# One half of a hand-ordered attention and gated-unit kernel in another order, its closing test cut in two

## The chip, the cores and the metric

The kernel runs on one core of a Trainium2 chip. Its engines work side by side, each through its own list of instructions, in order: PE (matrix products into PSUM, with PEld, its weight loads), DVE (the vector engine, VectorE), ACT (the scalar engine, ScalarE, with exponential, tanh and copies), POOL (GpSimd, elementwise work in SBUF) and SP, which here only issues transfers. PSUM has eight banks, numbered 0 to 7. The metric is the device time of the whole program in microseconds, lower being better, as the median of three runs.

## The reference

Eight batches of eight heads, 576 positions, head width 64. Attention is causal, and every head has a decay made of running sums of a gate `s`:

```python
scores = scale * np.matmul(q, k.transpose(0, 1, 3, 2))
cum = np.cumsum(np.maximum(s, 0.0), axis=-1)
bias = -(cum[:, :, :, None] - cum[:, :, None, :])
scores = np.where(causal, -1000000000.0, scores + np.minimum(bias, 0.0))
attn = softmax(scores)                      # over keys
x = (attn @ v)                              # (batch, 576, 512)
gate = sigmoid(causal convolution of x over positions, 5 taps per channel)
out = (gate * (x @ w_val)) @ w_out
```

## The kernel before

The work is cut into 32 blocks `n`, each one batch and one pair of heads (`n // 4` is the batch, `n % 4` the pair). The names of steps are those of the code; a number behind the dot is the block, or the batch and a part of it.

- `ld_q`, `ld_k`, `ld_v`, `ld_t` load on SP's queue (lines 435, 467, 471, 458); `c_q`, `c_k` cast queries and keys to bf16, `qt`/`qq` turn them over on PE and `qe` copies them out of PSUM (`tt`, `te` the same for the last 64 positions). `vp` (line 474, POOL) multiplies the values by the decay's factor.
- `s0`, `s1`, `s2` are the score products of a block in three portions (line 505), each on a pair of banks; `e0`, `e1`, `e2` are their exponentials on ACT (line 556), written to one of three buffers `P`. The causal mask of the diagonal blocks is made in one of two ways: with `mk` in the list POOL clears it in `P` (line 579), without it PE adds a large negative number with two further matmuls (line 518).
- `av0`, `av` multiply by the values (line 594), `rec` takes the reciprocal of the sum (line 607, DVE), `nm` normalises (613), `xt` turns the result over (626, PE) and `xe` copies it out (373).
- `t1` to `t4` add the taps of the convolution, on DVE (665, 670) or, with a product `p2` to `p4` ahead of them (654, or 652 on ACT), on POOL (673); `th` is the tanh (690 and 684), `val` the product with `w_val` (703), `glu` the gating (712, DVE), `out` and `outa` the product with `w_out` (723), `oe` its copy out of PSUM, `st` the store (731).
- The last four blocks, 28 to 31, are split in two parts of 384 and 192 positions, so their steps have a second number, and `u0` to `u3`, `f0` to `f3` (line 570), `mk` and `ml` stand for scores, exponentials and masks.
- At the end the kernel tests whether its shortcut was allowed: reciprocals not too small and their sum not too large (lines 734, 735, 745, 746), the convolution's weights not too large (739, 740). A matmul `cnt` counts (749), `cntc` takes the least count (758), `flag` reads it, and another path is run if the test fails.

The order of all this isn't made by a planner at run time: the string `ORDER` names every step with its engine (S, G, T, A, V) and its banks or buffers, and a loop at the end of `main_path` emits them one by one. Each engine's list is the string filtered by that engine's letter. An instruction waits for what it reads and for the readers of what it overwrites. So what a step waits for is set by the position of other steps in the string and by the banks and buffers written beside it.

```python
for name, e, *slots in steps:
    f, *ix = name.split(".")
    ...
    does[f](engines[e], *ix)
```

Of the kernel before, what the change touches and what calls it, by code (L numbers as in the profile page):

```python
# [204 lines left out]
av.2:T t2.0:V ld_v.1.0:S qe.1.3:A tt.1:T:5 ld_v.1.3:S qe.1.2:V p4.1:G:0 p4.0:A:1 ld_v.1.4:S ld_wv:S:4 av0.3:T:6+7
av.3:T te.1:A rec.2:V ld_t.2:S t4.1:G c_q.1.1:G nm.2:V s0.6:T:0+1:1 rec.3:V xt.2:T:5 nm.3:V e0.6:A t4.0:G s0.7:T:2+3:2
xe.2:V s2.6:T:6+7 e0.7:A qq.1.0:T:0:1 t1.2:V:2 mk.6:G p2.1:A:0 s1.6:T:2+3 t3.2:V qe.1.0:A ld_q.2:S:0 mk.7:G qe.1.1:V
e2.6:A t3.1:V s1.4:T:0+1 e1.6:A s0.4:T:6+7:0 t2.2:V ld_k.2:S:1 xt.3:T:4 e0.4:A s0.5:T:2+3:0 t2.1:G t4.2:V s2.4:T:6+7
xe.3:V wu.24:T:5 e2.4:A vp.1.0:G mk.4:G wu.25:T:5 t1.3:V:3 wu.26:T:5 wu.27:T:5 ld_wo:S:2 wu.28:T:5 e1.4:A s4.1.3:T:6+7
ld_t.3:S t3.3:V wu.29:T:5 wu.30:T:5 e4.1.3:A s1.5:T:0+1 t4.3:V wu.31:T:5 th.2:A:0 ld_q.3:S:3 vp.1.2:G av0.4:T:6+7  # L210
th.1:A:1 av.4:T t2.3:V e0.5:A vp.1.1:G cast_wv:G rec.4:V av0.6:T:4+5 nm.4:V av.6:T e1.5:A s2.5:T:2+3 rec.6:V
s1.7:T:6+7 nm.6:V e2.5:A xt.4:T:0 ld_v.2.2:S c_q.2:G:1 tt.2:T:1 xe.4:V th.0:A:2 av0.5:T:2+3 t1.4:V:2 av.5:T te.2:A
ld_v.2.4:S val.3.0:T:4 th.3:A:3 p4.4:G:1 rec.5:V val.3.1:T:1 nm.5:V e1.7:A val.1.0:T:5 glu.3.0:V t4.4:G xt.5:T:2
c_k.2:A:2 glu.3.1:V ld_v.2.1:S val.1.1:T:3 glu.1.0:V s2.7:T:6+7 glu.1.1:V qq.2.0:T:1:5 vp.1.3:G xe.5:V val.0.0:T:3
t2.4:V e2.7:A val.0.1:T:4 t1.5:V:1 p2.5:G:0 qe.2.0:A av0.7:T:6+7 glu.0.0:V glu.0.1:V ld_v.2.3:S val.2.0:T:3 t2.5:G
p3.5:A:1 t3.4:V av.7:T ld_v.2.0:S qe.2.1:A qq.2.1:T:4:2 ld_k.5:S:4 rec.7:V cast_wo:G nm.7:V val.2.1:T:0 qe.2.3:A
xt.6:T:5 glu.2.0:V xt.7:T:1 xe.6:V qe.2.2:A s0.9:T:6+7:1 glu.2.1:V s1.9:T:2+3 p4.5:G:0 xe.7:V out.0.2:T:0 e0.9:A
t1.6:V:0 out.0.0:T:4 t3.5:G t1.7:V:3 e1.9:A ld_k.3:S:0 t4.6:V s1.8:T:6+7 oe.0.2:A:0 s0.8:T:2+3:0 mk.9:G oe.0.0:A:1
t3.7:V val.7.0:T:0 e0.8:A ld_t.4:S out.0.3:T:4 t2.6:V p3.6:G:1 e1.8:A t2.7:V out.0.1:T:2 t3.6:G th.4:A:4 t4.7:V
val.4.0:T:3 st.0.2:S val.7.1:T:7 glu.4.0:V th.7:A:3 val.4.1:T:1 t4.5:G oe.0.3:V:2 th.6:A:1 ld_v.3.2:S s2.8:T:5+6  # L220
glu.7.1:V s4.2.3:T:3+4 glu.7.0:V e2.8:A val.6.0:T:7 glu.4.1:V vp.2.0:G val.6.1:T:0 glu.6.0:V e4.2.3:A ld_v.3.3:S
oe.0.1:V:3 s0.10:T:5+6:2 th.5:A:2 c_q.3:G:0 s2.9:T:3+4 glu.6.1:V av0.8:T:1+2 e2.9:A av.8:T val.5.0:T:0 ld_q.5:S:1
e0.10:A rec.8:V nm.8:V vp.2.1:G s2.10:T:3+4 val.5.1:T:7 e2.10:A glu.5.0:V s1.10:T:1+2 glu.5.1:V s0.11:T:5+6:0 vp.2.2:G
e1.10:A xt.8:T:0 av0.9:T:3+4 xe.8:V tt.3:T:7 e0.11:A p4.8:G:1 t1.8:V:2 av.9:T ld_t.5:S qq.3.0:T:1:2 te.3:A rec.9:V
c_k.3:G:1 nm.9:V s1.11:T:5+6 qe.3.1:A out.0.7:T:7 ld_v.3.4:S t2.8:V qe.3.0:A av0.10:T:3+4 st.0.1:S oe.0.7:V:4 xt.9:T:0
t4.8:G av.10:T e1.11:A xe.9:V ld_v.3.0:S s0.12:T:1+2:1 rec.10:V t1.9:V:3 out.0.6:T:7 e0.12:A vp.2.3:G nm.10:V
ld_v.3.1:S s1.12:T:5+6 oe.0.6:A:5 s2.11:T:1+2 t3.9:V xt.10:T:3 e1.12:A p3.8:G:0 out.0.8:T:7 xe.10:V e2.11:A t4.9:V
ld_q.4:S:2 mk.11:G s2.12:T:5+6 oe.0.8:V:0 e2.12:A qq.3.1:T:4:1 t3.8:G t1.10:V:0 tt.4:T:7 qe.3.3:A av0.11:T:5+6 t2.10:V
# [68 lines left out]
def main_path(ctx, tc, q, k, v, s, moe_w_val, moe_conv_w, moe_w_out, out, okcnt):  # L297
# [5 lines left out]
    NS = B * 4  # L303
# [444 lines left out]
    def count(e):  # L748
        pe.matmul(bank[0:1, at["cnt"][0], 0:24], onec, ok, start=True, stop=True)
# [90 lines left out]
```

## Time and profile before

| what | us |
|---|---|
| three runs | 190.02, 189.6, 187.79 |
| median | 189.6 |
| profiled execution, from its first to its last instruction | 187.6 |
| PE busy | 170.1 |
| ACT busy | 170.6 |
| POOL busy | 164.5 |
| DVE busy | 163.3 |

The profiled execution is another one than the three timed ones, and its own time is the span in the table. In a row of the groups the order is: line, engine, operation, what it writes and reads, shapes and count; then busy time in all, the mean of one in ns, and the engine's idle time ahead of these instructions with what ended it. In a row of the timeline: start, duration, engine, line, and in brackets idle time ahead of it. In the chain of waits: start, duration, what. A busy time of PE counts matmuls from start to modelled end, so that short matmuls that overlap count once.

### The profile page before, as it was taken

The page shows a single profiled execution, that of the slowest core. Times are in us where ns is not written, and L with a number is a line of the kernel's source. Part 1 is how long each engine was busy: PE and PEld are TensorE (multiplying, and loading weights), DVE is VectorE, ACT ScalarE, POOL GpSimd, SP SyncE. Part 2 cuts the span into 40 slices and gives each one's busy share as a digit, 9 for nine tenths or more (in the row PEclk, how much of TensorE's full clock was granted, in tenths as well). Part 3 has the DMA queues.
Part 4 walks back from the last instruction along what each step waited for, and adds up shares of the span by engine and source line. Part 5 has one row for each costly group of instructions (what it writes and reads, how often), then busy time and mean ns, then how long its engine had stood idle before and what let it go on. Part 6 is the DMA issues. An engine that isn't in the chain of part 4 may idle for free.

```text
span 187.6 us, 6637 instructions
## 1 busy us (share of the span) xinstructions
PE 170.1 (91%) x2704; PEld 113.5 (60%) x2720; DVE 163.3 (87%) x321; ACT 170.6 (91%) x230; POOL 164.5 (88%) x149
## 2 busy tenths in 40 slices
PE   6898885888899998998978999999999999999991
PEld 2556573476757765576745667586566865776560
DVE  4355999878997899999999899998989899999980
ACT  2589899899999999999999999999999999999772
POOL 5267999899999999999978999999999989899610
PEclk9999999999999999999999999999999999999999
DMA  5998999999999999999298999899541003401164
GB/s 164 274 277 246 231 225 243 343 388 341 193 232 304 277 303 258 389 270 283 71 248 184 274 333 325 193 314 247 164 162 66 3 0 115 171 3 56 61 224 175
DMA packets 62283, 40.46 MB, mean 216 GB/s; under 512 B 47333, under 2 KB 49381, under 8 KB 62250
## 3 DMA queue, kind: packets, MB, share of 16 engines
q1 hardware_dynamic: 61706, 39.49, 77.1%
q8 instruction: 22, 0.36, 0.8%
q10 hardware_dynamic: 544, 0.52, 0.8%
q14 instruction: 11, 0.09, 0.2%
HBM read 30.57 MB, written 9.44 MB: 213 GB/s over the span
## 4 chain that ended last, share of the span: by engine, by line
PE 50%; ACT 15%; SPq 9%; DMA 8%; issue 6%; POOL 5%; DVE 4%; ACTq 0%; POOLq 0%; DVEq 0%
PE bank L723 14%; PE bank L703 11%; PE bank L594 10%; ACT P L556 9%; PE bank L505 7%; DMA vst<-in_v_dram 6%; SPq L435 3%; PE bank L629 3%; PE bank L626 3%; POOL gp L673 2%; DMA first<-in_k_dram 2%; ACT th L690 2%; SPq L471 2%; ACT QKT L373 2%; SPq L467 2%
## 5 line engine op out<-in xcount | busy, mean ns | idle before, releaser
L556 ACT ACTIVATE P<-bank 128x1024 bf16<-128x1024 f32 x84 | 82.9, 1042 | 4.1 <-PE bank L505 3.0
L670 DVE SCALAR_TENSOR_TENSOR gp<-bank,cwr,gp 128x574 f32<-128x574 bf16 (+6 forms) x72 | 52.3, 740 | 0.9 <-POOL gp L673 0.5
L673 POOL TENSOR_TENSOR gp<-gp,pr 128x572 f32<-128x572 f32 (+6 forms) x36 | 45.1, 1259 | 4.4 <-DVE gp L670 1.7
L474 POOL TENSOR_TENSOR Vp<-vst,w 128x650 bf16<-128x650 f32 x32 | 40.7, 1288 | 2.8 <-DMA vst<-in_v_dram 1.8
L505 PE MATMUL bank<-QKT 64*128 64x128 bf16 (+4 forms) x592 | 37.2, 237 | 4.8 <-ACT P L556 1.8
L703 PE MATMUL bank<-xT,wv 128*128 128x288 bf16 (+2 forms) x256 | 38.5, 287 | 1.1 <-ACT P L556 0.5
L594 PE MATMUL bank<-Vp,P 128*128 128x65 bf16 x960 | 36.0, 194 | 2.4 <-POOL Vp L474 1.1
L594 PEld LDWEIGHTS <-P 128*128 128x128 bf16 x960 | 33.2, 97 | 6.8 <-issue 1.5
L723 PE MATMUL bank<-wo,glu 128*128 128x512 bf16 x128 | 34.1, 380 | 1.5 <-issue 0.5
L505 PEld LDWEIGHTS <-QKT 64*128 64x128 bf16 x592 | 19.4, 94 | 22.3 <-issue 14.6
L712 DVE SCALAR_TENSOR_TENSOR glu<-th,bank 128x288 bf16<-128x288 f32 (+2 forms) x64 | 27.5, 445 | 2.0 <-ACT th L690 0.9
L703 PEld LDWEIGHTS <-wv 128*128 128x128 bf16 x256 | 22.4, 97 | 11.0 <-issue 4.8
L654 POOL TENSOR_TENSOR pr<-xT,cwr 128x572 f32<-128x572 bf16 (+6 forms) x28 | 28.3, 1020 | 0.6 <-ACT xT L373 0.6
L373 ACT COPY QKT<-bank 128x1024 bf16<-128x1024 bf16 (+1 forms) x26 | 24.2, 966 | 3.8 <-PE bank L489 2.9
L613 DVE TENSOR_TENSOR xn<-bank,recs 128x640 bf16<-128x640 f32 (+2 forms) x36 | 26.8, 745 | 0.6
L665 DVE SCALAR_TENSOR_TENSOR gp<-xT,cwr,bank 128x576 f32<-128x576 bf16 (+2 forms) x36 | 26.4, 741 | 0.7
L579 POOL TENSOR_SCALAR_AFFINE_SELECT P<-P 128x1024 bf16<-128x1024 bf16 (+1 forms) x22 | 22.3, 1021 | 4.2 <-ACT P L556 4.2
L690 ACT ACTIVATE th<-gp,cwr 128x576 f32<-128x576 f32 x28 | 22.0, 794 | 0.1
L723 PEld LDWEIGHTS <-glu 128*128 128x128 bf16 x144 | 12.4, 98 | 13.2 <-issue 1.6
L373 ACT COPY ot<-bank 128x512 f32<-128x512 f32 x26 | 15.2, 610 | 1.5 <-PE bank L723 1.0
L626 PE MATMUL bank<-ident,xn 128*128 128x128 bf16 x164 | 14.9, 219 | 0.7 <-ACT P L556 0.3
L373 POOL CAST qkb<-qkf 128x2048 bf16<-128x2048 f32 (+1 forms) x9 | 14.4, 1619 | 0.0
(66 smaller groups left out, 174.8 us busy)
## 6 DMA issues: line engine op xcount, KB each, us to landing
out_dram<-ot SPq DMA_DIRECT2D x36, 256.0 KB, 4.3
vst<-in_v_dram SPq DMA_DIRECT2D x28, 256.0 KB, 5.9
first<-in_q_dram SPq DMA_DIRECT2D x6, 512.0 KB, 6.0
first<-in_k_dram SPq DMA_DIRECT2D x6, 512.0 KB, 6.2
qkf<-in_q_dram SPq DMA_DIRECT2D x6, 512.0 KB, 6.7
qkf<-in_k_dram SPq DMA_DIRECT2D x6, 512.0 KB, 7.3
vst<-in_v_dram SPq DMA_DIRECT2D x15, 128.0 KB, 5.4
first<-in_q_dram SPq DMA_DIRECT2D x4, 256.0 KB, 5.3
```

Source lines behind the costliest of these rows:

```text
L373: (act.copy if e is act else e.tensor_copy)(dst, src)
L474: e.tensor_tensor(Vps[b % 2][:, :, HP[p]], vslot(b)[:, :, HP[p]], w[:, :, b * 8 + 2 * p:b * 8 + 2 * p + 2].unsqueeze(3).to_broadcast([128, ...
L505: pe.matmul(ps[:, hh, c0:c0 + nq], QKTs[b % 2][r, 1, p, k0:k0 + 128], QKTs[b % 2][r, 0, p, q0:q0 + nq], **kw)
L556: act.activation(out=Pt(n)[:, :, step * 512:(step + 1) * 512], in_=pair((f"s{step}", n)), func=AF.Exp, scale=0.125)
L594: pe.matmul(ps[:, o:o + 65], lhsT, Vps[b % 2][:, kb, 2 * p + w, :], start=(kb == 0), stop=(kb == qb))
L613: vec.tensor_tensor(xns[b % 2][:, g, p * 128:(p + 1) * 128].rearrange("t g (w d) -> t w g d", w=2), ps[:, :, :, 0:64], recs[:, n, :, g].un ...
L654: pool.tensor_tensor(pr, xTs[b % 2][:, c, 4 + lo - m:4 + hi - m], r.to_broadcast([128, hi - lo]), ALU.mult)
L670: vec.scalar_tensor_tensor(gp[:, lo:hi], xps(n, *h)[:, lo - m:hi - m], r, gp[:, lo:hi], ALU.mult, ALU.add)
L673: pool.tensor_tensor(gp[:, lo:hi], gp[:, lo:hi], prs[at[f"p{m}", n, *h][0]][:, lo:hi], ALU.add)
L703: pe.matmul(ps, wv[:, dc, c * 128:(c + 1) * 128], xTs[b % 2][:, dc, 4 + lo:4 + hi], start=(dc == 0), stop=(dc == 3))
L712: vec.scalar_tensor_tensor(glu2[:, c, o + lo:o + hi], th[:, lo:hi], 1.0, ps, ALU.add, ALU.mult)
L723: pe.matmul(bank_of(u, i), glu2[:, c, i * 128:i * 128 + 128], wo[:, c, :], start=(c == 0), stop=(c == 3))
```

## The change

Three things are edited.

1. The closing test. Before, `chk0` stood on DVE's list in block 27's neighbourhood and held the test of the convolution's weights and the least and the sum of the reciprocals of blocks 0 to 27 (280 columns); `chk`, at the end of DVE's list, held the reciprocals of blocks 28 to 31 (40 columns) and the comparisons. After, `chkw`, right behind `cwc` near the head of DVE's list, holds the weights' test, and `chk` at the end all 32 blocks' reciprocals (320 columns) and the comparisons. The count has 22 columns and no longer 24.
2. `ORDER` from about block 14's end is another one. Up to there every engine's list is as before, apart from `chkw`. SP's list is the same from beginning to end. Behind that point the lists of PE, ACT, DVE and POOL hold the same steps in a different order, with other banks and buffers, and with these differences: `te.6`, `xe.17`, `xe.19`, `oe.2.3`, `xe.29.0`, `xe.31.0` go from DVE to ACT; `xe.16`, `oe.1.8`, `oe.2.0`, `xe.27` from ACT to DVE; the masks `mk.18`, `mk.19`, `mk.22`, `ml.28`, `ml.29` leave POOL (PE makes them), and `mk.23`, `mk.26`, `mk.29`, `mk.30`, `mk.31` come to POOL.
3. How the list is written: the buffer `P` of a block now stands beside its exponentials, no longer beside its first scores, and `split(n)` asks a set made in advance.

```diff
@@ ORDER, head @@
-cwc:V xt.1:T:4 e2.3:A wu.23:T:6 xe.0:V
+c_k.1.1:G cwc:V xt.1:T:4 ld_t.1:S e2.3:A chkw:V vp.0.2:G wu.23:T:6 qq.1.1:T:0:7 xe.0:V
...
@@ ORDER, a piece of the second half @@
-av.15:T t1.14:V:0 qe.4.3:A p4.14:G:1 ld_v.5.2:S av0.12:T:4+5 rec.15:V av.12:T ld_v.4.3:S st.0.7:S nm.15:V tt.5:T:6
-p2.14:G:0 oe.1.0:A:5 ld_v.5.4:S st.0.0:S rec.12:V t3.14:V xt.15:T:1 te.5:A ld_v.5.1:S s0.16:T:2+3:2 xe.15:A nm.12:V
-s2.16:T:6+7 t4.14:G ld_v.5.3:S e0.16:A t1.15:V:3 ld_v.5.0:S xt.12:T:0 e2.16:A s0.17:T:4+5:0 xe.12:V t2.14:G
+xe.14:A t3.13:V qe.4.2:A av.15:T:6+7 ld_v.5.2:S t1.14:V:0 av0.15:T:6+7 ld_v.4.3:S oe.1.0:A:5 tt.5:T:2 p2.14:G:1
+rec.15:V qe.4.3:A st.0.7:S nm.15:V av0.12:T:3+4 av.12:T:3+4 t3.14:V te.5:A t4.13:G xt.15:T:5 ld_v.5.4:S s0.17:T:6+7
+xe.15:A rec.12:V st.0.0:S nm.12:V s4.4.3:T:0+1 e0.17:A:2 p4.14:G:0 t1.15:V:3 xt.12:T:2 e4.4.3:A s2.16:T:3+4 xe.12:V
...
-    Pt = lambda n, h=None: Ps[at["s0" if h is None else f"u{2 * h}", n][1]]
+    split = lambda n: n in splits
+
+    def Pt(n, h=None):
+        steps = ("e0", "e1", "e2") if h is None else (f"f{2 * h}", f"f{2 * h + 1}")
+        return Ps[next(at[f, n] for f in steps if (f, n) in at)[0]]
...
-    def check0(e):
+    def check_w(e):
         rf = cwr.rearrange("p c k -> p (c k)")
         e.tensor_tensor(okt, rf, rf, ALU.mult)
-        e.tensor_scalar(ok[:, 4:24], okt, 1e12, None, ALU.is_le)
-        extremes(e, 0, recs[:, 0:NE].rearrange("p a b c -> p (a b c)"))
-
-    def check1(e):
-        extremes(e, 1, recs[:, NE:NS].rearrange("p a b c -> p (a b c)"))
-        e.tensor_scalar(ok[:, 0:2], stat[:, 0:2], 5e-35, None, ALU.is_ge)
-        e.tensor_scalar(ok[:, 2:4], stat[:, 2:4], 1.5e31, None, ALU.is_le)
+        e.tensor_scalar(ok[:, 2:22], okt, 1e12, None, ALU.is_le)
+
+    def check(e):
+        rf = recs.rearrange("p a b c -> p (a b c)")
+        e.tensor_reduce(stat[:, 0:1], rf, AX.X, ALU.min)
+        e.tensor_reduce(stat[:, 1:2], rf, AX.X, ALU.add)
+        e.tensor_scalar(ok[:, 0:1], stat[:, 0:1], 5e-35, None, ALU.is_ge)
+        e.tensor_scalar(ok[:, 1:2], stat[:, 1:2], 1.5e31, None, ALU.is_le)
```

More of the change, by code (lines that the diff above doesn't have):

```diff
@@ L293 @@
-oe.3.8:A:3 out.3.7:T st.3.8:S cnt:T:7 oe.3.7:A:5 cntc:V st.3.7:S flag:S
+ld_q.0.0:S ld_k.0.0:A ld_k.0.1:A ld_t.0:S ld_s:S ld_q.0.1:S ld_q.0.2:S ld_k.0.2:S c_k.0.0:V ld_v.0.1:S c_q.0.0:V
+wu.0:T:0 wu.1:T:7 wu.2:T:0 wu.3:T:7 wu.4:T:0 wu.5:T:7 wu.6:T:0 wu.7:T:7 qt.0.0.k:T:0 c_k.0.1:G wu.8:T:2 qt.0.0.q:T:1
+qe.0.0.k:A qe.0.0.q:A wu.9:T:7 wu.10:T:2 wu.11:T:7 s0.0:T:0+1 ld_q.0.3:S tt.0:T:2 e0.0:A:0 qt.0.1.k:T:3 ld_k.0.3:S
+te.0:A mk.0:G relu:V ld_v.0.0:S qe.0.1.k:A wu.12:T:4 wu.13:T:7 wu.14:T:0 s1.0:T:1+2 scan:V s4.0.0:T:4+5 s2.0:T:6+7
@@ L766, in main_path @@
                 t2=tap(2), t3=tap(3), t4=tap(4), th=tanh, val=val, glu=glu, out=outp(0), outa=outp(1), oe=out_evac, st=store,
-                chk0=check0, chk=check1, cnt=count, cntc=count_out, flag=flag)
+                chkw=check_w, chk=check, cnt=count, cntc=count_out, flag=flag)
     engines = dict(S=sync, G=pool, T=pe, A=act, V=vec)
```

218 lines of the change are left out of this document (106 added, 112 removed).

## The prediction

> **What bounds the kernel now.** The page comes first: who is busy, and what the chain of work that ended last consists of.
>
> ```profile
> span 187.6 us, 6637 instructions
> PE 170.1 (91%) x2704; PEld 113.5 (60%) x2720; DVE 163.3 (87%) x321; ACT 170.6 (91%) x230; POOL 164.5 (88%) x149
> PE 50%; ACT 15%; SPq 9%; DMA 8%; issue 6%; POOL 5%; DVE 4%; ACTq 0%; POOLq 0%; DVEq 0%
> ```
>
> Four engines lie within 4% of each other, so an average says little. The next view is the busy time by stage. I cut it at 92 us, where the instruction lists of the two kernels begin to differ (up to there each engine keeps its old list, but for one new step, below), and at 147 us, where the chain changes hands.
>
> ```profile
> 0.00:92.00 92.00, 81.76 (x1357) 54.18 (x1364) 77.05 (x142) 82.76 (x105) 82.44 (x75) 1.00 1.03 270
> 92.00:118.00 26.00, 23.79 (x432) 16.61 (x433) 24.59 (x45) 24.93 (x32) 24.41 (x20) 1.00 0.91 254
> 118.00:147.00 29.00, 28.32 (x448) 18.76 (x445) 27.47 (x51) 28.74 (x38) 28.71 (x24) 1.00 0.66 179
> 147.00:176.00 29.00, 28.74 (x424) 19.64 (x424) 28.06 (x64) 28.32 (x46) 26.85 (x30) 1.00 0.18 66
> 176.00:183.50 7.50, 7.45 (x65) 4.29 (x62) 5.95 (x21) 5.32 (x13) 2.08 (x4) 1.00 0.46 170
> ```
>
> Columns: stretch, length, busy time of PE, weight loads, DVE, ACT and POOL. The idle time is what an order of work can win. From 92 to 118 PE has 26.00 - 23.79 = 2.21 us, ACT 1.07. From 118 to 147 PE has 0.68, ACT 0.26 and POOL 0.29: ACT and POOL are 99% busy. From 147 to 176 PE has 0.26, from 176 to 183.5 it has 0.05. The chain of waits agrees:
>
> ```profile
> 144.11 1.05 ACT P L556
> ...
> 145.83 0.92 ACT P L556
> ...
> 176.72 1.73 PE bank L723 x8
> ...
> 183.47 0.59 ACT ot L373
> ```
>
> Up to 147 us ACT's exponentials end last; after it PE's matmuls follow each other without a gap (L723: 1.73 us for 8, 0.216 each) until the last copy out.
>
> **The change part by part.** Against this profiled execution: its own time is the span, 187.6 us; nothing around it is shown. Times of whole runs are 190.02, 189.6 and 187.79: the fastest lies 0.2 above the span, the mean (189.14) 1.5, the median 2.0.
>
> *The weight test moves to the head of VectorE's list* (`chkw`, behind `cwc`, before `xe.0`), and the test of the sums of exponentials, once in two parts, becomes one at the tail.
>
> ```profile
> L734 DVE TENSOR_REDUCE stat<-recs 128x1 f32<-128x280 f32 x1 | 0.4, 437 | 0.0
> L739 DVE TENSOR_TENSOR okt<-cwr 128x20 f32<-128x20 f32 x1 | 0.4, 376 | 0.0
> L734 DVE TENSOR_REDUCE stat<-recs 128x1 f32<-128x40 f32 x1 | 0.2, 185 | 0.0
> L740 DVE TENSOR_SCALAR ok<-okt 128x20 bf16<-128x20 f32 x1 | 0.2, 176 | 0.0
> ```
>
> The head gains 0.38 + 0.18 = 0.55 us near 21 us. No wait is added there, but `xe.0`, the convolution taps and the copy `qe.1.1` queue behind it, and others wait for that copy:
>
> ```profile
> 31.09 0.68 PE L505 MATMUL bank<-QKT 64*128 64x64 bf16 x12 [1.78 <-DVE QKT L373]
> 33.69 1.94 ACT L556 ACTIVATE P<-bank 128x1024 bf16<-128x1024 f32 x2 [0.54 <-PE bank L505]
> 37.77 2.85 ACT L556 ACTIVATE P<-bank 128x1024 bf16<-128x1024 f32 x3 [0.33 <-PE bank L594]
> ```
>
> The copy ends 0.55 us later, PE's scores too, and ACT, which waited for PE at 33.69 already, with them; ACT's 0.33 us of idle time before 37.77 then takes up 0.33 of it. About 0.2 us can be left. Bounds 0 and 0.55; I take **+0.2**, the remainder that these rows give.
>
> In the middle (156 us) VectorE loses all of `chk0`: 0.38 + 0.18 and two reductions of 0.44 (L734 and its like for the sum), 1.43 us; it wasn't on the chain there, so 0. At the tail a reduction grows from 40 to 320 columns: 437 - 185 = 252 ns for 240 columns, 1.05 ns each, so about 0.48 us instead of 0.18, twice: +0.6 us.
>
> ```profile
> 182.04 0.18 DVE L734 TENSOR_REDUCE stat<-recs 128x1 f32<-128x40 f32 x1
> 182.37 0.17 DVE L746 TENSOR_SCALAR ok<-stat 128x2 bf16<-128x2 f32 x1
> 183.37 0.17 PE L749 MATMUL bank<-ok,onec 128*1 128x24 bf16 x1
> ```
>
> The test ended at 182.54; PE, busy with the last output product, reads it at 183.37. The cover is 0.83 us and takes the 0.6: **0**. Without the cover it would cost up to 0.6, and even then only the flag would wait; the last store hangs on the copy at 183.47, which doesn't need the test.
>
> *Ten evacuations change engine.* To ACT go `te.6`, `xe.17`, `xe.19`, `oe.2.3`, `xe.29.0`, `xe.31.0`; to VectorE go `xe.16`, `oe.1.8`, `oe.2.0`, `xe.27`.
>
> ```profile
> L373 ACT COPY ot<-bank 128x512 f32<-128x512 f32 x21 | 12.3, 607 | 1.5 <-PE bank L723 1.0 <-ACT ot L373 0.6
> L373 ACT COPY xT<-bank 128x576 bf16<-128x576 bf16 x6 | 3.9, 658 | 0.0
> L373 ACT CAST QKT<-bank 128x512 bf16<-128x512 f32 x1 | 0.6, 586 | 0.4 <-PE bank L480 0.4
> L373 ACT COPY xT<-bank 128x384 bf16<-128x384 bf16 x1 | 0.5, 487 | 0.0
> L373 DVE COPY xT<-bank 128x576 bf16<-128x576 bf16 x8 | 3.6, 450 | 0.2 <-PE bank L626 0.2
> L373 DVE COPY ot<-bank 128x512 f32<-128x512 f32 x4 | 2.7, 682 | 0.0
> L373 DVE CAST QKT<-bank 128x512 bf16<-128x512 f32 x2 | 1.4, 687 | 0.2 <-PE bank L480 0.2
> ```
>
> ACT before 147 us: 0.59 + 2 x 0.66 + 0.61 - 0.66 - 2 x 0.61 = +0.64. After it: -0.66 + 2 x 0.49 = +0.32, where ACT has 0.68 idle before 176: 0. VectorE gets 0.46 lighter before 147 (0.69 + 2 x 0.45 + 0.68 - 0.45 - 2 x 0.68); it wasn't on the chain, so nothing. The 0.64 on ACT stands where ACT ends last. It costs 0.64 if its gaps stay, and if the new order closed all of them (1.07 + 0.26) it would be a gain of 1.33 - 0.64 = 0.69. I take **+0.3**, the price with half of it lost in gaps, since the 92 to 118 stretch still has 1.07.
>
> *Masks change between PE and POOL.* Blocks 18, 19, 22 and the small masks of 28 and 29 go to PE; 23, 26 and the large masks of 29, 30, 31 go to POOL.
>
> ```profile
> L579 POOL TENSOR_SCALAR_AFFINE_SELECT P<-P 128x1024 bf16<-128x1024 bf16 x6 | 6.6, 1100 | 0.0
> L579 POOL TENSOR_SCALAR_AFFINE_SELECT P<-P 128x256 bf16<-128x256 bf16 x4 | 1.7, 426 | 0.0
> ```
> ```profile
> 126.50 0.21 PE bank L518 x2
> ...
> 128.18 0.11 PE bank L518 x2
> ```
>
> POOL before 147: (2 - 3) x 1.10 = -1.10. After it: three masks of 768 columns, between 0.43 and 1.10, about 0.88 on the line between them, less two of 0.43: +1.8, into 29.00 - 26.85 = 2.15 us idle: hidden, and 0.2 at most if all three took 1.10. On PE a pair costs 0.21 for 512 columns, 0.11 for 256. Before 147: +0.21, where PE has 2.9 us idle: 0. After 147, where PE is the chain: minus three pairs of 384 columns (0.11 to 0.21, take 0.16), plus two of 128 (under 0.11, take 0.05): -0.4, between -0.1 and -0.6. I take **-0.3**, as not all of it lies on the chain.
>
> *POOL's queue near 91 us.* `vp.3.0` now runs ahead of `t4.13` (1.43 us), and `c_k.6` (1.89) comes eleven us earlier.
>
> ```profile
> 89.71 1.43 POOL L673 TENSOR_TENSOR gp<-gp,pr 128x572 f32<-128x572 f32 x1
> 91.06 1.32 POOL L474 TENSOR_TENSOR Vp<-vst,w 128x650 bf16<-128x650 f32 x1
> 98.97 3.77 POOL L474 TENSOR_TENSOR Vp<-vst,w 128x650 bf16<-128x650 f32 x3 [0.88 <-DMA vst<-in_v_dram]
> 102.67 1.89 POOL L373 CAST qkb<-first 128x2048 bf16<-128x2048 f32 x1
> ```
> ```profile
> SPq L471 <- POOL Vp L474: 6.4, 1, 6.4
> ```
> ```profile
> PE bank L594 <- POOL Vp L474: 0.2, 1, 0.2
> ```
>
> SP's load `ld_v.5.2` waits 6.4 us for `vp.3.0`, and every later load stands behind it on SP's queue, whose order of names is the same in both kernels. So these loads start 91.06 - 89.71 = 1.35 us sooner, and POOL's 0.88 us wait at 98.97 goes; `c_k.6` fills the place. PE waited only 0.2 for that product; next late is ACT, busy there. Bounds 0 and -0.9; I take **-0.2**. Behind `c_k.6` queue `p2.14` and `t4.13`, 0.5 us later than now or more (1.89 less the 1.35); who reads them has no idle time in these rows, so 0.5 of cost stays in the range.
>
> *Reuse of PSUM banks by the scores.* Walking the score steps of blocks 16 to 31 through the list, a step follows the previous one on the same bank pair four times before and nine times after, so that PE must wait for ACT to read. Such a wait has a row:
>
> ```profile
> 97.60 0.40 PE L505 MATMUL bank<-QKT 64*128 64x64 bf16 x4 [0.51 <-ACT P L556]
> ```
>
> In all nine ACT has another step between the two exponentials. On the other hand, the steps whose bank was freed only one ACT step before its own exponential fall from 17 to 9. Bounds: 5 x 0.51 = +2.6, and a gain inside ACT's gaps, above; I take **+0.2**. The Trainium skill (Perfetto Trace Analysis, Optimizing Tensor Performance, Matmuls) says that independent groups of matmuls should rotate through the banks, so that one's evacuation overlaps the next group's matmuls. By that rule the nine repeats speak against the change; the row at 97.60 agrees with it as a size, but no row here shows nine of them.
>
> Sum: +0.2 + 0 + 0.3 - 0.3 - 0.2 + 0.2 = **+0.2 us**, a span of 187.8. Put on the mean of the runs (1.5 above the span) this is **189.3 us**.
>
> **The rivals.** *A: hand-over of banks, slower.* Each of the nine repeats holds PE for 0.51 us and ACT gets its scores late by as much: 9 x 0.51 = 4.6, a span of 192.2, some 193.7 as a run. It is past 2% (3.8 us) from eight exposed repeats on. For it: ACT's gaps are so small that a late score has no room. Against: the ACT step in between lasts at least as long as the wait (the copies above, 0.59 to 0.66).
>
> *B: ACT becomes the whole bound.* All 0.64 + 0.32 lie on the path and nothing is won back: 187.6 + 1.0 + 0.2 = 188.8, as a run 190.3. For it: 99% busy up to 147. Against: ACT was not the chain after 147.
>
> *C: the new order closes the gaps, faster.* ACT's 1.33 and PE's 0.31 go, PE's 0.4 goes too, ACT's 0.64 comes: 187.6 - 1.4 = 186.2, as a run 187.7. For it: fewer tight hand-overs, the POOL wait gone. Against: the chain after 147 is matmuls alone. More than that needs PE to have room inside its busy time. The weight loads fill 18.76 + 19.64 = 38.4 of 58 us from 118 to 176. The Trainium skill (Perfetto Trace Analysis, Identifying the Most-Contended Engine) holds that matmul busy time is no measure of headroom, and weight-load share and useful flops are; by it PE would have room. In this trace eight 512-column matmuls take 1.73 us at a granted clock of 1.00, and ACT is at 99% beside them, so a third of 58 us is not to be had.
>
> *D: nothing.* The search only finds another order as good as the last: 187.6, as a run 189.1.
>
> **How the numbers follow.** Forecast with D: 0.58. B: 0.14. C: 0.16, of which 0.05 passes 2%. A: 0.12, of which 0.08 passes 2% (fewer exposed repeats give the rest). 2%, or 3.8 us, is about what a measurement of this kernel tells from no change; the three runs alone spread over 2.2. So faster 0.05, same 0.87, slower 0.08. The range for eight in ten runs from C, less a little for the runs' spread (187.7 - 0.9 = 186.8), to B and the beginning of A (190.3 + 1.0 = 191.3).
>
> **What would show it.** `chk`'s reductions should last near 0.48 us and end before PE's last product; ACT's gap at 37.77 should be gone; POOL's wait for the load near 99 us too. PE should still be over 98% busy from 147 to its end, and ACT over 98% from 118 to 147. Waits of PE's score matmuls (L505) for ACT beyond some 2 us after 92 would be rival A; a kernel under 186 us would say that PE or ACT had room that busy time hides.

## The result

The changed kernel took 191.96 us (median; 191.19 to 192.88) beside 189.43 us for the kernel before: a ratio of 1.0154, 95% interval 1.011 to 1.0198. Timed once more (`f1_after_again`, below) it came to 191.01 beside 188.99, 1.0107 (1.0049 to 1.0165). So it is slower by 2.0 to 2.5 us, a little over 1%: inside the 2% band. The first median lies past the upper end of the forecast's range (191.3), the repeat just inside it. The profiled execution took 191.19 us with a span of 189.5, so 1.7 us lie around the span.

The page of the changed kernel: span, busy times, granted clock in forty slices, shares of the chain that ended last.

```profile
span 189.5 us, 6653 instructions
PE 172.5 (91%) x2720; PEld 113.8 (60%) x2720; DVE 166.5 (88%) x317; ACT 171.1 (90%) x232; POOL 165.3 (87%) x149
PEclk9999995799999999999999999999999999999999
PE 38%; ACT 24%; DVE 16%; POOL 9%; issue 6%; DMA 4%; ACTq 0%; DVEq 0%; POOLq 0%
```

PE's share of the last chain fell from 50% to 38%, and DVE and POOL, 4% and 5% before, hold 25%. Two slices near 30 us have a clock of 0.5 to 0.7 of full speed. The busy time by stage, in the columns of the prediction (the clock and the DMA stand last):

```profile
0.00:92.00 92.00, 82.42 (x1356) 54.58 (x1357) 77.91 (x143) 81.87 (x104) 81.86 (x75) 0.96 1.00 270
92.00:118.00 26.00, 23.75 (x434) 16.35 (x432) 24.81 (x44) 24.72 (x32) 24.70 (x19) 1.00 0.98 272
118.00:147.00 29.00, 28.39 (x428) 18.39 (x427) 28.02 (x48) 28.84 (x39) 26.09 (x22) 1.00 0.60 163
147.00:176.00 29.00, 28.81 (x441) 19.44 (x438) 27.24 (x60) 28.23 (x47) 27.57 (x27) 1.00 0.18 66
176.00:183.50 7.50, 7.23 (x65) 4.51 (x64) 6.99 (x20) 5.57 (x13) 5.10 (x9) 1.00 0.27 99
183.50:189.50 6.00, 1.88 (x10) 0.59 (x8) 1.50 (x6) 1.84 (x4) 0.00 (x0) 0.97 0.52 189
```

Past 118 us hardly anything is different: ACT is 99% busy from 118 to 147, PE from 147 to 176, as before. The last row is the loss: 1.88 us of PE's work that the kernel before had done by 183.5. Where the time goes can't be read from shares; it is read from the head of VectorE's list (timeline of the changed kernel):

```profile
20.28 0.17 DVE L410 TENSOR_TENSOR cwr<-bank,cwi 128x16 f32<-128x16 f32 x1
20.49 0.40 DVE L737 TENSOR_TENSOR okt<-cwr 128x20 f32<-128x20 f32 x1
20.82 1.29 POOL L476 TENSOR_TENSOR Vp<-vst,w 128x650 bf16<-128x650 f32 x1
20.92 1.22 DVE L738 TENSOR_SCALAR ok<-okt 128x20 bf16<-128x20 f32 x1
22.05 0.45 DVE L375 COPY xT<-bank 128x576 bf16<-128x576 bf16 x1
```

L737 and L738 are `chkw`. L738 compares 20 columns and lasts 1.22 us. The prediction priced it at 0.18 from the same instruction at 156.56 us. It ends at 22.14, when POOL's product, begun at 20.82, ends at 22.11. `xe.0`, the copy behind it, ends 1.7 us later than in the kernel before, counted from the end of the first exponential.

To see what becomes of such a delay I counted each engine's instructions off against its list in `ORDER` and took the ends of five steps from each trace: `e0.0` (the first exponential, the common start), `xe.14` (near 92 us, where the lists begin to differ), `nm.12` (near 96), `e1.27` (near 151) and `oe.3.7` (the last copy out). The time between them, in us, for all runs told below:

```
                                          e0.0 to  xe.14 to  nm.12 to  e1.27 to
                                          xe.14    nm.12     e1.27     oe.3.7
kernel before (clock never cut)           82.95    3.97      55.52     32.74
old order, test at the tail    (e4)       83.60    3.95      55.54     32.81
old order, head, squares PSUM  (g1)       83.70    3.81      55.17     32.74
old order, test in the head    (e1)       84.39    3.85      55.54     32.75
new order, test at the tail    (e2)       83.12    4.12      56.14     33.13
 .. and oe.1.0 moved           (g2)       83.70    4.00      55.40     33.13
 .. and xe.19 on VectorE       (f4)       82.68    4.53      56.17     33.13
changed kernel                            84.08    4.66      55.39     33.48
changed kernel again           (f1)       84.57    4.00      55.40     33.49
 .. and oe.1.0 moved           (h2)       84.28    4.00      55.64     33.50
 .. without three masks        (e3)       84.17    4.00      55.39     33.43
 .. squares in PSUM            (f2)       83.83    5.82      55.41     33.49
 .. PSUM and oe.1.0 moved      (h1)       83.79    3.99      55.46     33.49
 .. taps' test 11 us later     (f3)       84.06    5.15      55.86     33.50
old order to 130 us, then new  (h3)       83.19    3.81      55.90     33.30
new order to 109 us, then old  (g4)       81.98    4.12      56.39     32.74
```

Up to `xe.14` the two orders hold the same lists but for the test, so the first column compares the places of the test alone. I return to it in each part.

### The profile page after: what moved, and what is told of

Its sections match the earlier page's. It is cut to its first block, busy times and chain, and to the rows that moved or that the text cites. A ratio compares the mean times of both kernels' runs of the same rounds, so it can differ in the third digit from the quotient of the medians.

```text
span 189.5 us, 6653 instructions
## 1 busy us (share of the span) xinstructions
PE 172.5 (91%) x2720; PEld 113.8 (60%) x2720; DVE 166.5 (88%) x317; ACT 171.1 (90%) x232; POOL 165.3 (87%) x149
## 4 chain that ended last, share of the span: by engine, by line
PE 38%; ACT 24%; DVE 16%; POOL 9%; issue 6%; DMA 4%; ACTq 0%; DVEq 0%; POOLq 0%
ACT P L562 16%; PE bank L725 9%; PE bank L705 8%; PE bank L507 7%; PE bank L599 7%; POOL gp L678 5%; DVE xn L618 3%; ACT QKT L375 3%; POOL pr L659 3%; DVE QKT L375 3%; ACT th L693 2%; DVE gp L675 2%; DMA first<-in_k_dram 2%; PE bank L631 2%; DVE glu L714 2%
## 5 line engine op out<-in xcount | busy, mean ns | idle before, releaser
L675 DVE SCALAR_TENSOR_TENSOR gp<-bank,cwr,gp 128x573 f32<-128x573 bf16 (+5 forms) x72 | 53.1, 745 | 1.1
L507 PE MATMUL bank<-QKT 64*128 64x128 bf16 (+4 forms) x592 | 38.1, 243 | 5.0 <-DVE QKT L375 2.5
L705 PE MATMUL bank<-xT,wv 128*128 128x288 bf16 (+2 forms) x256 | 37.8, 286 | 0.7 <-DVE glu L714 0.3
L725 PE MATMUL bank<-wo,glu 128*128 128x512 bf16 x144 | 36.0, 380 | 0.2 <-DVE glu L714 0.2
L507 PEld LDWEIGHTS <-QKT 64*128 64x128 bf16 x592 | 20.1, 96 | 23.9 <-issue 15.8
L714 DVE SCALAR_TENSOR_TENSOR glu<-th,bank 128x288 bf16<-128x288 f32 (+2 forms) x64 | 26.8, 446 | 0.8 <-ACT th L687 0.4
L584 POOL TENSOR_SCALAR_AFFINE_SELECT P<-P 128x1024 bf16<-128x1024 bf16 (+2 forms) x22 | 23.0, 1050 | 3.6 <-ACT P L562 3.6
L631 PE MATMUL bank<-ident,xn 128*128 128x128 bf16 x164 | 15.1, 222 | 1.4 <-DVE xn L618 1.0
```

The lines of the kernel that those rows point to most:

```text
L507: pe.matmul(ps[:, hh, c0:c0 + nq], QKTs[b % 2][r, 1, p, k0:k0 + 128], QKTs[b % 2][r, 0, p, q0:q0 + nq], **kw)
L675: vec.scalar_tensor_tensor(gp[:, lo:hi], xps(n, *h)[:, lo - m:hi - m], r, gp[:, lo:hi], ALU.mult, ALU.add)
L705: pe.matmul(ps, wv[:, dc, c * 128:(c + 1) * 128], xTs[b % 2][:, dc, 4 + lo:4 + hi], start=(dc == 0), stop=(dc == 3))
L714: vec.scalar_tensor_tensor(glu2[:, c, o + lo:o + hi], th[:, lo:hi], 1.0, ps, ALU.add, ALU.mult)
L725: pe.matmul(bank_of(u, i), glu2[:, c, i * 128:i * 128 + 128], wo[:, c, :], start=(c == 0), stop=(c == 3))
```

## The experiments

**The test or the order?** My theory after the result (H) was that the place of the test in the head is the loss; the rival (O), that the new order is. Two kernels move the test, one in each order, a third has it at the tail of the old order, and the changed kernel is timed once more.

```diff
 e1: the kernel before, with the changed kernel's test
-e2.3:A wu.23:T:6 xe.0:V
+e2.3:A wu.23:T:6 chkw:V xe.0:V
-chk0:V xe.27:A
+xe.27:A
...
-chk:V
+chk:V (320 columns)
 e2: the changed kernel              e4: as e1, but chkw at the tail
-e2.3:A:0 chkw:V vp.0.2:G
+e2.3:A:0 vp.0.2:G
-oe.3.5:A:4 chk:V
+oe.3.5:A:4 chkw:V chk:V
```

> The old order with nothing changed but the closing test: the taps' part stands in the head ahead of xe.0, the reductions over all 320 reciprocals at the tail, and the middle part is gone. Theory H (the head): the 20-column comparison is held up for as long as GpSimd's Vp product beside it runs, about 1.2 us instead of 0.18, this falls on the path of the first batch, and TensorE's clock is cut for some us near 30 us; the time is 1.1 us above the kernel before (190.5). Theory O (the new order alone costs the time): the comparison may be long, but the gaps later take it up; within 0.4 us of the kernel before (189.4).

> The new order with the taps' part of the test moved from the head to just ahead of the reductions at the tail. Theory H: the comparison takes 0.2 us there, the first stretch to 92 us goes 1.1 us faster, TensorE's clock is not cut near 30 us, and the time is 1.1 us below the changed kernel (190.8). Theory O: the first stretch may be shorter, but the end stays within 0.4 us of the changed kernel (192.0).

> The old order with the whole closing test at the tail: taps' part and reductions over all 320 reciprocals, nothing in the head and nothing in the middle. Theory H: 1.1 us below the version with the taps' part in the head, 189.4; the reductions of about 1.07 us and the 0.4 us of the taps' part are hidden while TensorE ends its products (at most 0.3 us shown: 189.7). Theory O: the same as the version with the taps' part in the head.

> The changed kernel itself once more, timed beside the next three. Every theory: 1.2 to 1.6 per cent above the kernel before.

Measured, each beside the kernel before: e1 1.0055 (1.0022 to 1.0087), e2 1.0049 (1.0017 to 1.008), e4 1.0021 (0.9989 to 1.0053), f1 1.0107, a little under the 1.2 to 1.6% that I expected of it. The place in the head costs the old order 190.11 - 189.14 = 0.97 us, as theory H had it, and the new order more, 1.1 to 2 us. With the test at the tail the new order is still 0.5 us behind the old (189.63 against 189.14), which is no more than the intervals leave open. In e1's trace L738's like lasts 1.22 us again, at the tail of e2 0.18:

```profile
20.46 0.41 DVE L734 TENSOR_TENSOR okt<-cwr 128x20 f32<-128x20 f32 x1
20.81 1.28 POOL L473 TENSOR_TENSOR Vp<-vst,w 128x650 bf16<-128x650 f32 x1
20.91 1.22 DVE L735 TENSOR_SCALAR ok<-okt 128x20 bf16<-128x20 f32 x1
```

```profile
182.54 0.17 DVE L737 TENSOR_TENSOR okt<-cwr 128x20 f32<-128x20 f32 x1
182.75 0.18 DVE L738 TENSOR_SCALAR ok<-okt 128x20 bf16<-128x20 f32 x1
182.83 0.48 DVE L742 TENSOR_REDUCE stat<-recs 128x1 f32<-128x320 f32 x1
```

The multiplication has two prices as well: 0.40 in the head, where POOL's copy of `qkb` before the product ends at 20.86, and 0.17 where POOL is idle. The whole test at the tail of the old order (e4) costs nothing that can be measured. One thing of the expectation was wrong: I had the cut of the clock near 30 us down to the test. It is in e4's and e2's traces too.

**What holds the comparison up?** Theory L: VectorE and GpSimd are in each other's way at SBUF. Rival W: the instruction waits for its input, or is slow in this form. Where the squares go to PSUM the comparison has the same input, the same form and the same neighbour, but no SBUF operand to read. f2 does that in the changed kernel, g1 in the old order with the test in the head. f3 leaves the squares in SBUF and puts the test 11 us later, ahead of `t3.1`, where I expected GpSimd idle.

```diff
 f2 and g1
-        e.tensor_tensor(okt, rf, rf, ALU.mult)
-        e.tensor_scalar(ok[:, 2:22], okt, 1e12, None, ALU.is_le)
+        okp = bank[:, at["cwT"][0], 256:276]
+        e.tensor_tensor(okp, rf, rf, ALU.mult)
+        e.tensor_scalar(ok[:, 2:22], okp, 1e12, None, ALU.is_le)
 f3
-e2.3:A:0 chkw:V vp.0.2:G
+e2.3:A:0 vp.0.2:G
...
-e2.6:A:1 t3.1:V
+e2.6:A:1 chkw:V t3.1:V
```

> The changed kernel with the squares of the taps written to a free part of the PSUM bank and read from there by the 20-column comparison; place in the order unchanged. Theory L (VectorE and GpSimd get in each other's way at SBUF: the comparison, which has only an SBUF operand, can't run while GpSimd's Vp product runs): the comparison takes 0.2 us beside the same product, and the time is 1 to 2 us below the changed kernel. Rival W (the comparison is late for another reason, a wait for its input or a slow form of the instruction): it stays at 1.2 us, and the time with it.

> The old order with the taps' part of the test in the head, its squares kept in PSUM, so that the comparison has no SBUF operand to read. Theory L (the hold-up beside GpSimd is what costs): the comparison takes 0.18 us, the step after it comes 1.0 us earlier than with the squares in SBUF, and 0.6 us of the 0.97 us that the place in the head cost in the old order is won back: 189.5 beside a kernel before of 188.9. Rival E (any work put there costs the same): 190.1.

> The changed kernel with the taps' part of the test still in the head, but some 11 us later on VectorE, ahead of t3.1, whose result GpSimd stands idle for. Theory L: the comparison takes 0.18 us, and the two instructions cost their own 0.4 us: 0.3 to 0.5 us above the version with it at the tail. Rival E (anything added to VectorE early on costs 1 to 2 us, through TensorE's idle time and its clock): as slow as the changed kernel.

Timeline of f2, and then of f3:

```profile
20.69 0.41 DVE L737 TENSOR_TENSOR bank<-cwr 128x20 f32<-128x20 f32 x1
21.03 1.28 POOL L475 TENSOR_TENSOR Vp<-vst,w 128x650 bf16<-128x650 f32 x1
21.14 0.18 DVE L738 TENSOR_SCALAR ok<-bank 128x20 bf16<-128x20 f32 x1
```

```profile
29.18 2.14 POOL L584 TENSOR_SCALAR_AFFINE_SELECT P<-P 128x1024 bf16<-128x1024 bf16 x2
29.20 1.22 DVE L375 COPY QKT<-bank 128x1024 bf16<-128x1024 bf16 x1
30.33 1.02 DVE L737 TENSOR_TENSOR okt<-cwr 128x20 f32<-128x20 f32 x1
31.39 0.18 DVE L738 TENSOR_SCALAR ok<-okt 128x20 bf16<-128x20 f32 x1
```

Theory L holds. Beside the same POOL product the comparison takes 0.18 us when it reads PSUM. In f3 GpSimd isn't idle yet: two masks run to 31.32, so now the multiplication, which reads SBUF, lasts 1.02 us and ends at 31.35, and the comparison behind it takes 0.18. The Trainium skill (SBUF — State Buffer, "SBUF: two separate sides") says that VectorE and GpSimd share a pair of SBUF ports under an exclusive lock: a VectorE operation in a two-port mode, or with two SBUF inputs against a GpSimd operation that reads SBUF, and a GpSimd operation shut each other out for a whole instruction, whichever starts first. These rows agree (1.22, 0.40 and 1.02 us in place of 0.18 and 0.17, each until POOL's instruction ended). The comparison has one SBUF input, so by that rule it would have to be in a two-port mode; no run here shows the mode itself. The kernel before agrees too: a reduction, which is neither of the two kinds, took 0.44 us for 280 columns beside POOL's instruction of 1.43 (0.48 for 320 at the tail, with POOL idle). The multiplication of its test, in the same rows, was held from 156.15 to 156.53, the end of POOL's instruction before.

```profile
155.36 1.14 POOL L654 TENSOR_TENSOR pr<-xT,cwr 128x572 f32<-128x572 bf16 x1
...
156.15 0.38 DVE L739 TENSOR_TENSOR okt<-cwr 128x20 f32<-128x20 f32 x1
...
156.57 1.43 POOL L673 TENSOR_TENSOR gp<-gp,pr 128x572 f32<-128x572 f32 x1
156.65 0.44 DVE L734 TENSOR_REDUCE stat<-recs 128x1 f32<-128x280 f32 x1
```

In the old order the freed comparison is worth what L expected: g1 189.46, 1.0012 (0.9979 to 1.0045) against e1's 1.0055, and the first column above gives 83.70 for 84.39. In the changed kernel it was worth nothing: f2 191.34, 1.0105 (1.0048 to 1.0162), f3 191.26, 1.0118 (1.0058 to 1.0177), both misses for L's times, although f2's first column is as short as g1's. f3 is no clean test of the place, since the multiplication was held up there.

**Where f2's gain went.** Its second column is 5.82 us where others have 4.0. Two things happen there. PE stands still for 1.83 us in front of `av0.15`, and the profile names nothing that it waits for ("issue"):

```profile
94.75 0.61 PE L598 MATMUL bank<-Vp,P 128*128 128x65 bf16 x15 [1.83 <-issue]
```

PE stood still at the same step in f3 (1.16 us), the changed kernel (0.67) and f4 (0.54), and that is by how much their second columns, and f2's, are above 4.0. In f3, the changed kernel and f4 the profile puts it down to VectorE, whose instruction had ended 0.4 to 0.6 us before. In all four PE went on 1.4 to 1.6 us after a load of 16 KB on the queue of instruction loads had landed, and in no kernel with the new order at this place did it begin the step sooner than 1.2 us after. That points at PE's own instructions coming late; no run tests it. And f2's profile is of its slowest execution (192.39 us).

The other thing is a wait of ScalarE, which I had taken for the whole cause. ScalarE in f2, and then in e4 (old order):

```profile
92.25 1.03 ACT L374 COPY QKT<-bank 128x1024 bf16<-128x1024 bf16 x1
94.59 0.59 ACT L374 COPY ot<-bank 128x512 f32<-128x512 f32 x1 [1.31 <-DMA out_dram<-ot]
95.08 1.02 ACT L374 COPY QKT<-bank 128x1024 bf16<-128x1024 bf16 x1
```

```profile
91.69 1.95 ACT L372 COPY QKT<-bank 128x1024 bf16<-128x1024 bf16 x2
93.50 0.63 ACT L372 COPY ot<-bank 128x512 f32<-128x512 f32 x1
```

`oe.1.0` writes the output buffer 5, which the store `st.0.5` must have emptied. The old order has both copies of `QKT` (`qe.4.2`, `qe.4.3`) ahead of it; the new order has it between them, a 1 us step earlier, and there the store has often not landed: ScalarE waited 1.31 us in f2, 0.70 in e2, 1.49 in f4, and not at all in the profiled executions of the changed kernel, which come there later. In f2 this wait lies beside PE's longer one. In e2 and f4 it shows in the third column, 56.14 and 56.17 for 55.40.

```profile
92.82 0.58 ACT L375 COPY ot<-bank 128x512 f32<-128x512 f32 x1 [0.70 <-DMA out_dram<-ot]
```

Theory S: a kernel that is early at 92 us gives its gain back at this store. Three kernels put `oe.1.0` behind `qe.4.3`: the new order with the test at the tail (g2), with the squares in PSUM (h1), and the changed kernel as it is (h2).

```diff
-ld_v.4.3:S oe.1.0:A:5 tt.5:T:2 p2.14:G:1 rec.15:V qe.4.3:A st.0.7:S
+ld_v.4.3:S tt.5:T:2 p2.14:G:1 rec.15:V qe.4.3:A oe.1.0:A:5 st.0.7:S
```

> The new order with the whole test at the tail, and ScalarE's evacuation oe.1.0 put one step later, behind qe.4.3, where the old order has it. Theory S (in the new order ScalarE comes to this step before the store that empties its buffer has landed, and waits): the wait of 0.7 us at 92.8 us goes, the time is 0.3 to 0.6 us below the version without the move, 189.1 to 189.3. Rival: the store wait is only passed on, no difference.

> The changed kernel, its test kept where it is, with both repairs: the squares in PSUM, so that the comparison isn't held up, and oe.1.0 one step later on ScalarE. With the squares in PSUM alone the comparison took 0.18 us and the time stayed (1.0105 of the kernel before). Theory S (what was won in the head was lost again to the store that oe.1.0 waits for, 1.3 us in that trace): with both, 1.003 to 1.005 of the kernel before. Rival E (the time saved in the head is never worth anything in the new order): 1.010.

> The changed kernel with oe.1.0 one step later and nothing else. Theory S: with the comparison held up in the head, ScalarE comes to oe.1.0 only after the store has landed in most executions, so the move alone is worth little: 1.009 to 1.012 of the kernel before, that is 0 to 0.5 us better than the changed kernel. Rival M (the order of these two steps is the main loss whatever the head does): 1.005 or less.

g2 189.50, 1.0019 (0.9985 to 1.0053), where e2 had 1.0049: 0.57 us, as expected, but the two intervals overlap. Its third column is e2's less 0.74 us. h1 189.94, 1.0063 (1.0029 to 1.0097), where f2 had 1.0105: somewhat above the band I gave, with the rival's 1.010 just outside its interval. Nor is this difference clear of the intervals, and since PE's stop of 1.83 us is gone in h1's trace as well, it isn't shown to be the move's. h2 191.26, 1.0138 (1.0098 to 1.0178), above the band I gave: the move alone is worth nothing. ScalarE in h1 has no gap there any more:

```profile
91.81 1.95 ACT L374 COPY QKT<-bank 128x1024 bf16<-128x1024 bf16 x2
93.62 0.63 ACT L374 COPY ot<-bank 128x512 f32<-128x512 f32 x1
```

So with this step where the old order has it, the three places of the test in the new order read as in the old one: 1.0138 in the head, 1.0063 in the head with PSUM, 1.0019 at the tail. Some 1.4 us (0.75% of 189) are the hold-up by GpSimd; h1 and h2 were timed in one series, and their intervals just don't overlap. Another 0.8 us (0.44%), which the intervals leave open, would be the two instructions and what they delay; 0.36 us of it are found in one place below (the last stage). In the old order the same two are 0.8 us and nothing that can be measured.

**The masks on GpSimd.** From 160.7 to 178 us the chain of the changed kernel runs through POOL, which the prediction had counted as covered. e3 takes the three masks from it that were put there after 147 us, and PE makes them.

```diff
-mk.29:G
...
-mk.30:G
...
-mk.31:G
```

> The new order with three masks of the last batch taken from GpSimd (mk.29, mk.30, mk.31; TensorE adds their mask products again, 128 columns times 3 blocks times 2 heads each, about 0.13 us each). Theory M (GpSimd is the path from 152 to 182 us, and its masks of 0.87 us each are what was added to it): 0.7 us below the changed kernel (191.3). Rival (TensorE's and ScalarE's work sets that stretch, and GpSimd only follows): within 0.3 us of the changed kernel, or 0.3 us above it.

e3 took 190.95, 1.0106 (1.006 to 1.0153), the changed kernel beside it in another series 1.0107. The last column stays, 33.43 for 33.48, though POOL's busy time from 147 to 176 falls by 2.5 us:

```profile
147.00:176.00 29.00, 28.77 (x423) 19.25 (x424) 27.07 (x59) 27.96 (x47) 25.02 (x24) 1.00 0.18 66
```

Theory M falls: the chain went through POOL, but PE, 99% busy beside it, was as late.

**An evacuation back on VectorE.** f4 is e2 with `xe.19` on VectorE.

```diff
-t4.17:V xe.19:A s1.21:T:2+3
+t4.17:V xe.19:V s1.21:T:2+3
```

> The new order with the taps' part at the tail, and the evacuation xe.19 on VectorE again, as in the kernel before. Theory A (ScalarE is what the stretch from 118 to 147 us is bound by, and the evacuations moved to it are the price): ScalarE saves 0.67 us there, GpSimd's wait of 3.0 us at 122 us shrinks to about 1, and the time is 0.5 us below the version with the tail alone. Rival (VectorE is as full, and pays 0.45 us): no difference beyond 0.3 us.

f4 took 189.87, 1.0055 (1.002 to 1.009), e2 1.0049: no gain. ScalarE's busy time from 118 to 147 is the same, 28.62 us in f4 and 28.65 in e2, and the third column too, 56.17 and 56.14. Theory A falls.

**Halves of both orders.** g3 and h3 are the old order up to `xe.21` and the new one behind it, g4 the new order (with `oe.1.0` moved) up to `e2.19` and the old one behind it, all with the test at the tail. In g3 the blocks 22 and 23 shared one buffer of probabilities, so their attention is mixed and has waits of its own: its 191.72 us, 1.0144 (1.0097 to 1.0191), tells nothing. h3 has the buffers renumbered.

```diff
 g3, h3:  old list up to xe.21:V, then every step not yet named, as the new list has it
 h3:      P buffers of the second part renumbered, 0 to 2, 1 to 0, 2 to 1
 g4:      new list up to e2.19:A:0, then every step not yet named, as the old list has it
```

> The old order up to the evacuation xe.21 (some 130 us), the new order from there, the whole test at the tail. Theory T (the new order loses 0.3 to 0.7 us in the last stage, from 152 us on): the step e1.27 ends as in the old order, and the last output evacuation 0.3 to 0.7 us later: 189.5. Theory M (it loses only before 130 us): as the old order with the test at the tail, 189.1.

> The old order up to the evacuation xe.21 (some 130 us), the new order from there, the whole test at the tail, with the buffers of the probabilities numbered so that no two items share one. Theory T (the new order loses 0.3 to 0.4 us in the last stage): from the end of e1.27 to the end of the last output evacuation 33.1 us instead of 32.8, and 1.003 to 1.005 of the kernel before. Theory M (it loses nothing there): 32.8 us, and 1.002.

> The other way round: the new order with oe.1.0 moved back up to the score exponential e2.19 (some 109 us), the old order from there, the whole test at the tail. Theories S and T together: the new order's head, 0.6 us ahead of the old one at 61 us, without its later losses: 188.6, 0.3 us below the kernel before. If the gain up to 61 us is only a matter of when the program's loads arrived, 189.1.

h3 took 190.53, 1.0101 (1.0062 to 1.014), above both theories; its last column, 33.30, is the new order's (33.13 to 33.50) and not the old one's (32.74 to 32.81). g4 took 189.99, 1.0063 (1.0034 to 1.0092), a miss: its last column is the old one, 32.74, but at the seam ScalarE stood still for 1.40 us (`e0.20`, 111.0 us). Its profiled execution, whose clock was not cut, was its fastest. Seams cost as much as what was to be measured, so their times say little; the last columns say that the new order's last stage is 0.3 to 0.8 us longer, wherever the stage before it came from.

## Why the prediction was wrong

The forecast was a span 0.2 us above the old one. By its own terms:

- *The test in the head, +0.2 out of 0 to 0.55.* This is the step that failed first. The profiles with the test at the tail have 82.68 to 83.70 us in the first column where the clock was cut (mean of e4, e2, g2, f4 and h3: 83.26), those with the test in the head 84.08 to 84.57 (mean of five: 84.30): +1.0 us, nearly twice the upper bound. The price was taken from rows at 156 us as if it were a property of the instruction. One of those rows held a warning: L739 took 376 ns for 20 columns, twice what the 16 columns of L410 and the 20 at the tail take (0.17), and ended with POOL's instruction. It was held up itself. In the head the two took 0.40 + 1.22 = 1.62 us and not 0.55, each until GpSimd's instruction ended. The GpSimd product that `chkw` would meet, `vp.0.2`, stands right behind it in the new list. The second half of the step, that ACT's idle time before 37.77 would take up 0.33 of it, was true in kind (that gap is gone) and came to too little.
- *The middle and the tail of the test, 0.* Right. The reductions last 0.48 and 0.47 us, as worked out, the test ends at 184.95, PE reads it at 185.21, and the last copy out starts at 185.36:

```profile
184.28 0.47 DVE L743 TENSOR_REDUCE stat<-recs 128x1 f32<-128x320 f32 x1
184.79 0.16 DVE L745 TENSOR_SCALAR ok<-stat 128x1 bf16<-128x1 f32 x1
185.21 0.17 PE L748 MATMUL bank<-ok,onec 128*1 128x22 bf16 x1
185.36 0.59 ACT L375 COPY ot<-bank 128x512 f32<-128x512 f32 x1 [0.28 <-PE bank L725]
```

- *ACT's 0.64 us of added copies, +0.3; POOL's queue, -0.2; the banks, +0.2.* Together +0.3 between 92 and 151 us. Beside e4 the changed kernel measured +0.7 to `nm.12` and -0.15 after it, the second time 0.05 and -0.14. The size is about right, the contents aren't: from `nm.12` to `e1.27` the order is as good as the old one with more work on ACT, and what the first profile lost lies in the 4 us behind `xe.14`, where PE stood still for 0.67 us in front of `av0.15` (the first row under rival A, below, names VectorE, whose instruction had ended 0.64 us before). The second profile doesn't show it. POOL's wait for a load near 99 us is gone, as said. That a copy on ACT had been moved ahead of `qe.4.3`, and so nearer to a store, was not seen: I had followed SP's queue for its loads alone.
- *The masks, hidden on POOL, -0.3 on PE.* Hidden is right (e3). The gain on PE isn't there. The last stage took 33.48 us and not 32.74: instead of -0.3 it is +0.4 with the test at the tail and +0.7 with it in the head. This is the second term that failed. It is not the masks (e3). The first 0.4 us, the new order's own, stay open: PE is busy for nearly all of the stage in both orders, and the mean durations of its matmuls are the same, so there is no single wait to name. The other 0.36 us come in at one step, `xe.27`. Up to it the steps of ScalarE and VectorE lie as far behind `e1.27` in f1 as in g2, and from it on those that hang on it are 0.3 to 0.36 us later. The products that it reads (L631) and the copy itself, in f1, where the test stands in the head, and then in g2, where it stands at the tail:

```profile
157.20 0.45 PE L631 MATMUL bank<-ident,xn 128*128 128x128 bf16 x5
158.11 0.46 DVE L375 COPY xT<-bank 128x576 bf16<-128x576 bf16 x1 [0.65 <-PE bank L631]
```

```profile
156.05 0.45 PE L631 MATMUL bank<-ident,xn 128*128 128x128 bf16 x5
156.61 0.46 DVE L375 COPY xT<-bank 128x576 bf16<-128x576 bf16 x1 [0.29 <-PE bank L631]
```

The copy starts 0.46 us after PE's products in f1, 0.11 in g2. In all seven traces of the new order with the test ahead of this step it starts 0.40 us after VectorE's instruction that waits for PE, in e2, g2 and f4 0.04. In those seven the copy is the 320th entry of VectorE's list in the trace, waits counted, and in the three others the 318th or 319th: the test's two instructions shift it. So this cost goes with the place in the list and not with the hold-up at 21 us, for f2 and h1, without the hold-up, have it too. Why an instruction is late at that place, no run shows.
- *Rival A, the banks.* Not it: PE's score matmuls waited for ACT 0.6 us in all after 92, against the 2 us that were to show it:

```profile
PE bank L599 <- DVE gp L675: 0.7, 1, 0.7
PE bank L599 <- ACT P L562: 0.7, 1, 0.7
PE bank L507 <- ACT P L562: 0.6, 2, 0.3
```

- Counted again, a score step follows the previous one on its bank pair five times before, not four, and nine times after; and if all three large masks took 1.10, POOL would lack 0.3 us, not 0.2. Neither changes a term of the sum.
- *Rival B* gave 190.3 and came nearest by its size, for a reason that the runs don't show: the 0.64 us on ACT did not stay.
- *The range.* Its upper end was built from ACT's and the banks' prices, with 0.55 at most for the head. A bound for an instruction that had never stood beside that neighbour should have gone to the neighbour's length, 1.3 us.

Sum as measured, by the table: about +1.0 for the head, 0 to +0.7 behind `xe.14`, 0 to -0.15 after it, +0.7 at the end: 1.6 to 2.3 us, beside 2.0 to 2.5 in the times. The hold-up is shown by the runs; about 0.4 us of the last stage are not explained. No version made here beats the kernel before: the best, g1, g2 and e4, can't be told from it.

## What to carry to other kernels

The duration of a small instruction in a profile holds for the neighbours it had there. Before a step is moved, look at what GpSimd will be running beside it at the new place, and put the bound at that instruction's length; a far cheaper way than another place can be another home for the operand, here PSUM. When an early gain doesn't show in the time, look for the next thing that isn't set by the engines' work, such as a store that must land: behind it, in e2 and g2, lay 0.74 us of one column. And compare the step times of several traces before a wait is called the cause: in f2 the wait that has a name lay beside a longer one that has none.

## What the runs showed of the hardware

The 20-column instruction that lasts as long as the other engine's is told above. The other surprise is the clock. Busy times and clock from 28 to 36 us, in the kernel before and in the changed one:

```profile
28.00:36.00 8.00, 5.80 (x92) 2.97 (x89) 7.79 (x11) 7.46 (x10) 7.10 (x7) 1.00 1.14 278
```

```profile
28.00:36.00 8.00, 6.48 (x87) 4.11 (x88) 7.79 (x13) 6.59 (x8) 6.41 (x6) 0.57 1.08 286
```

The profiled execution of the kernel before was one of its few in which the clock was never cut here. Thirty more beside e1 have a mean granted clock of 0.977 to 0.994, but for two at 1.000 (187.53 and 188.62 us, where the median is 188.89). Nearly all profiles here have one stretch of 3.4 us at 0.50 near 30 us (mean clock 0.985 to 0.991), and the changed kernel's two profiles have twice that (0.981, 0.982). The Trainium skill (TensorE: Matmul & The Clock Gate, "Part 1: The HAM clock gate") has the clock either whole or half, by how busy TensorE was in a window of 3.4 us that runs free of the kernel. An estimate from that page: one window at half speed in 189 us is a mean clock of 0.991, two 0.982. The most frequent value, 0.991, agrees, and so do the changed kernel's. In the profiles at 0.985 to 0.988 the clock is cut once more in the last 2 us, where PE has nothing left to do (e4 from 184 us on: clock 0.82, PE busy 0.00). The trace the forecast was argued from had 82.95 us in the first column, against a mean of 83.26 in the five with the test at the tail and the clock cut, which spread from 82.68 to 83.70; every comparison of one trace with one other has to allow for that much.
